# Infini-attention plus SiLU MLP: two input tiles loaded in halves on two queues, VectorE's constants made later, 39 idle products for 44

## The chip, the core and the metric

The kernel runs on one core of a Trainium2 chip. TensorE (PE, with its weight loads as PEld), VectorE (DVE), ScalarE (ACT), GpSimd (POOL) and SyncE (SP) each work through an order of their own; DMAs are issued by SP and ACT and carried by 16 DMA engines. The metric is device time in microseconds, lower is better. Three runs of the kernel before took 222.0, 222.07 and 222.56 us, median 222.07.

## What is computed

The input x is 2048 rows of 512 bf16 values. Each row is normed (mean and variance), and the normed rows go through an attention with memory and through a dense block; both results are added to x.

```
xn  = layernorm(x)
q, k, v = xn @ wq, xn @ wk, xn @ wv            # 32 heads of 16, 4 segments of 512 rows
a_dot = softmax(q k^T * scale + causal mask) v   # inside a segment
a_mem = (phi(q) M) / (phi(q) z)                # M, z: sums over the segments before
out = x + (g * a_mem + (1 - g) * a_dot) @ wo + silu(xn @ w1) @ w2
```

## The kernel before, in words

The rows are cut into 16 tiles of 128 rows, four to a segment. The order of all work is written out by hand in the string ORDER (L16 to L90): each word names a piece with its numbers, a table at L839 maps it to a function, and a loop at the end emits the pieces one after the other. Nothing reorders them; each engine gets its own instructions in that order and waits on semaphores only.

The first line of ORDER is the start of the kernel, and it is what the change touches. Its words, as far as they matter here:

- `kind`, `odd`, `omask` (L232, L217, L229): eight small VectorE instructions that make constants of one column: which rows are even or odd heads (pm_odd, pm_even), and masks worked out from them. pm_odd and pm_even are first read by GpSimd at L376, in the copy of the first keys; the others much later.
- `ones0`, `ones1`, `zeros`: memsets of GpSimd.
- `xc`t, `xd`t (L279, L283): the statistics of tile t on VectorE and their aggregation; `xq`t (L297) a square root on ACT, `xi`t (L300) the reciprocal, `Nv`t (L308) the normed tile xn_t, both on VectorE.
- `busy`n (L833): n idle products on PE, 128x128 by 128x128, of zeros; they read zraw, which VectorE's first memset fills, and write a bank that nobody reads. `busy44` stands ahead of the first turn, `busy6` behind it.
- `X`t`.1` (L812): four transposes of xn_t on PE into PSUM, and `Xa`, `Xv` (L819) their copies to xnT by ACT (tiles 0 and 1) or VectorE (tiles 2 and 3).
- `v0.0.`n, `v0.1.`n (L386): the value products of tiles 0 and 1, one product per word, which read wv; `k0.`, `q0.` (L365, L380) the keys and queries of the first segment, which read wk and wq and all four tiles; `tb` (L303) loads ACT's table for the exponential.
- `h` (L470): the dense block's products, which read w1.

Ahead of the loop, the function issues the input DMAs (L163 to L180). Tile 0 goes on SP's queue and tile 1 on ACT's, then tile 2 on SP's and tile 3 on ACT's; then SP issues wv in two parts, wk, wq, four tiles of x, w1, and the other eight tiles. A DMA's end is counted on one of eight counters, given out in turn: the ninth DMA of the program takes over that of an early one and is issued only once that one has ended. In the kernel before the ninth is the load of tiles 4 to 7 (x_hi), which waits for tile 1.

On VectorE the start is: memset of zraw (L183), memset of the lower half of lows (L257), the eight constants, then the statistics of tile 0. On ACT: two DMA issues, the load of the square root's table with a small activation (L185), then the square root of tile 0.

Of the kernel before, what the change touches and what calls it, by code (L numbers as in the profile page):

```python
# [13 lines left out]


ORDER = """  # L16
kind odd omask ones0 ones1 zeros xc0 xd0 xc1 xq0 xi0 Nv0 busy44 xd1 xq1 xc2 xi1 X0.1 Nv1 xd2 Xa0.1 busy6 v0.0.0 v0.0.1 xq2 X1.1 Xa1.1 xs3 v0.0.2 v0.0.3 xq3 v0.1.0 xi2 v0.1.1 v0.1.2 v0.1.3 Nv2 xi3 X2.1 va0.0 va0.1 Nv3 Xv2.1 X3.1 Xv3.1 k0.0.0 k0.0.1 k0.1.0 k0.0.2 k0.0.3 k0.3.0 q0.0.0 q0.0.1 q0.0.2 q0.0.3 ka0.0 fp0.0 qv0.0 tb fa0.0 q0.2.0 k0.1.1 k0.1.2 k0.1.3 kv0.1 fp0.1
S0 q0.1.0 q0.1.1 q0.1.2 q0.1.3 k0.3.1 xs4 xs6 xs7 xs5 xg4.4 q0.2.1 q0.2.2 qa0.1 q0.2.3 qv0.2
S2 v0.2.0 v0.2.1 k0.3.2 k0.3.3 kv0.3 fa0.1 v0.3.0 v0.3.1 v0.3.2 Nv7 v0.2.2 XD7 v0.2.3
S1 Nv5 vv0.2 h0.5.0 h0.10.0 h0.10.1 h0.10.2 v0.3.3 vv0.3 xs8 Nv6 XD6 h0.5.1 h0.5.2 XD5 h0.5.3 ha0.5  # L20
# [73 lines left out]
def kernel(  # L94
# [13 lines left out]
    nc = tc.nc  # L108

    P = 128  # L110
# [14 lines left out]
    x_flat = A_x.flatten_outer_dims()  # L125
# [18 lines left out]
    def xs(t0, t1):  # L144
        if t0 >= NT - TPS:
            return x_end[:, t0 - NT + TPS : t1 - NT + TPS, :]
        return x_lo[:, t0:t1, :] if t1 <= TPS else x_hi[:, t0 - TPS : t1 - TPS, :]
# [6 lines left out]
    wo_sb = cpool.tile([P, DT, D], BF16, name="wo_sb")  # L154
    beta_r = cpool.tile([P, 1], BF16, name="beta_r")

    def load_x(eng, t0, n):
        eng.dma_start(
            out=xs(t0, t0 + n),
            in_=x_flat[t0 * P : (t0 + n) * P, :].rearrange("(n p) d -> p n d", p=P),  # L160
        )

    load_x(nc.sync, 0, 1)  # L163
    load_x(nc.scalar, 1, 1)
    load_x(nc.sync, 2, 1)
    load_x(nc.scalar, 3, 1)
    def load_w(eng, w_sb, W, k0, k1):
# [11 lines left out]
        out=beta_r[:], in_=bass.AP(tensor=A_beta.tensor, offset=A_beta.offset, ap=[[1, H], [0, 4], [1, 1]])  # L179
# [9 lines left out]
    for i in range(2):  # L189
# [6 lines left out]
        out=b16[:], in_=ones8[:], compare_op=ALU.is_ge, fill=0.0,  # L196
# [3 lines left out]
        out=b16[:], in_=b16[:], compare_op=ALU.is_ge, fill=0.0,  # L200
# [9 lines left out]
    kind = cpool.tile([P, 1], F32, name="kind")  # L210
# [16 lines left out]
    omask = cpool.tile([P, 1], I32, name="omask")  # L227
# [687 lines left out]
```

## Time and profile before

| | us |
|---|---|
| median of three runs | 222.07 |
| the profiled execution's own time | 222.15 |
| its span, first to last instruction | 220.4 |
| PE busy, sum over the span | 214.9 (97%) |
| ACT busy | 184.0 (83%) |
| DVE busy | 179.7 (82%) |
| POOL busy | 135.1 (61%) |

The profile is that of one execution. Times in it count from the first instruction, so the 1.75 us between span and time lie around it. A row of the timeline has start, length, engine, line of the kernel, operation, tile written and tiles read, how many were merged, and in brackets how long the engine was idle before and what released it. SPq and ACTq are the queues that issue DMAs. In the rows on DMA queues stand packets, MB and the share of 16 engines; q1 is SP's queue and q10 ACT's. In the row of an instruction group, three numbers in ns are the least, median and greatest duration.

### The profile page before, as it was taken

How to read it: one execution, taken by the hardware profiler on the slowest of the kernel's cores; microseconds unless marked ns; L12 is line 12 of the kernel's file. 1: busy time of each engine (PE TensorE's matmuls, PEld its weight loads, DVE VectorE, ACT ScalarE, POOL GpSimd, SP SyncE). 2: the span in 40 equal slices, each digit the busy share in tenths (PEclk: the TensorE clock that was granted, in tenths of full speed). 3: DMA queues.
4: the chain of work that ended last, by engine and by line, in shares of the span. 5: the costliest groups of instructions: out<-in, count | busy, mean ns of one | idle time of the engine just before them, and what ended most of it. 6: DMA issues, size and time to landing. Idle time of an engine off the chain costs nothing.

```text
span 220.4 us, 9441 instructions
## 1 busy us (share of the span) xinstructions
PE 214.9 (97%) x4057; PEld 117.2 (53%) x4057; DVE 179.7 (82%) x368; ACT 184.0 (83%) x173; POOL 135.1 (61%) x253
## 2 busy tenths in 40 slices
PE   7999999999999999999999999999999999999994
PEld 7666645655553444454544444455454544455662
DVE  7789999988889788776897888969789887579554
ACT  3699999999999999999998999999989997971000
POOL 6089667997769976876669696693756364320000
PEclk9999999999999999999999999999999999999999
DMA  5993549552014221223303130142242020232313
GB/s 183 373 385 87 74 27 304 106 77 58 21 28 122 88 59 29 50 51 76 102 17 95 40 96 4 28 92 59 52 120 64 15 76 7 75 94 68 109 51 97
DMA packets 32746, 19.61 MB, mean 89 GB/s; under 512 B 14656, under 2 KB 32192, under 8 KB 32704
## 3 DMA queue, kind: packets, MB, share of 16 engines
q1 hardware_dynamic: 30080, 16.39, 28.6%
q10 hardware_dynamic: 2624, 2.62, 3.9%
q8 instruction: 31, 0.51, 1.0%
q14 instruction: 11, 0.09, 0.2%
HBM read 9.96 MB, written 2.10 MB: 55 GB/s over the span
## 4 chain that ended last, share of the span: by engine, by line
PE 79%; ACT 10%; DVE 4%; POOL 4%; issue 2%; POOLq 0%
PE ps L331 21%; PE psO L333 16%; PE ps L333 13%; PE psS L701 10%; PE psO L331 9%; ACT Pb L707 7%; PE psV L763 6%; PE psS L333 4%; POOL Pb L718 2%; DVE xn_t L310 1%; POOL lows L718 1%; ACT ex L408 1%; ACT th L477 1%; PE psM L437 1%; DVE stats L281 1%
## 5 line engine op out<-in xcount | busy, mean ns | idle before, releaser
L707 ACT ACTIVATE Pb<-psS 128x2048 bf16<-128x2048 f32 x72 | 135.2, 1878 | 7.5 <-PE psS L701 6.4
L718 POOL TENSOR_SCALAR_AFFINE_SELECT Pb<-Pb 128x256 bf16<-128x256 bf16 (+2 forms) x120 | 66.1, 571 | 22.3 <-ACT Pb L707 19.5
L482 DVE SCALAR_TENSOR_TENSOR hT<-th,ps 128x512 bf16<-128x512 bf16 x56 | 37.7, 679 | 9.1 <-ACT th L477 8.5
L718 POOL TENSOR_SCALAR_AFFINE_SELECT lows<-Pb 64x256 bf16<-64x256 bf16 (+1 forms) x56 | 26.7, 490 | 27.7 <-ACT Pb L707 25.3
L333 PE MATMUL psO<-w_sb,hT 128*32 128x512 bf16 (+2 forms) x716 | 42.5, 319 | 0.0
L331 PE MATMUL ps<-xnT,w_sb 128*128 128x512 bf16 (+1 forms) x160 | 35.2, 334 | 0.0
L477 ACT ACTIVATE th<-ps 128x512 bf16<-128x512 f32 x56 | 33.0, 598 | 2.2 <-PE ps L333 2.1
L333 PEld LDWEIGHTS <-hT 128*32 128x32 bf16 x884 | 21.8, 96 | 14.0 <-issue 3.3
L333 PE MATMUL ps<-xnT,w_sb 128*32 128x512 bf16 (+1 forms) x480 | 27.1, 341 | 0.1
L701 PE MATMUL psS<-qT,k 32*128 32x64 bf16 (+3 forms) x512 | 23.0, 233 | 0.8 <-ACT Pb L707 0.3
L331 PE MATMUL psO<-w_sb,hT 128*128 128x512 bf16 (+2 forms) x87 | 22.7, 334 | 0.0
L701 PEld LDWEIGHTS <-k 32*128 32x128 bf16 x512 | 9.8, 92 | 23.2 <-issue 21.7
L763 PE MATMUL psV<-Pb,Vz 128*32 128x448 bf16 (+7 forms) x512 | 21.6, 286 | 0.3 <-POOL Pb L718 0.3
L331 PEld LDWEIGHTS <-w_sb 128*128 128x128 bf16 x160 | 14.9, 98 | 12.1 <-issue 1.6
L763 PEld LDWEIGHTS <-Vz 128*32 128x32 bf16 x768 | 16.5, 97 | 9.1 <-issue 1.1
L376 POOL TENSOR_SCALAR k<-kT,pm_odd 128x512 bf16<-128x512 bf16 x16 | 12.0, 748 | 8.0 <-ACT kT L373 7.0
L333 PEld LDWEIGHTS <-w_sb 128*32 128x32 bf16 x480 | 11.9, 96 | 7.3 <-issue 1.9
L331 PE MATMUL ps<-wv_sb,xnT 128*128 128x512 bf16 x56 | 15.1, 381 | 0.2
L701 PE MATMUL psS<-qT,kT 16*128 16x448 bf16 (+3 forms) x256 | 14.7, 269 | 0.0
L333 PE MATMUL psO<-wo_sb,oT 128*32 128x512 bf16 x156 | 14.4, 380 | 0.0
L331 PE MATMUL ps<-xnT,wk_sb 128*128 128x256 bf16 (+1 forms) x64 | 13.6, 326 | 0.0
L793 DVE CAST oraw<-psV 128x512 bf16<-128x512 f32 x16 | 11.0, 689 | 3.0 <-PE psV L763 2.9
(110 smaller groups left out, 321.2 us busy)
## 6 DMA issues: line engine op xcount, KB each, us to landing
spr<-rz SPq DMA_DIRECT2D x56, 64.0 KB
x_res<-in_A_x_dram SPq DMA_DIRECT2D x16, 128.0 KB
out_dram<-o_out SPq DMA_DIRECT2D x15, 128.0 KB
w_sb<-in_B_w_dram SPq DMA_DIRECT2D x1, 1792.0 KB
w_sb<-in_B_w_dram ACTq DMA_DIRECT2D x1, 1792.0 KB
x_hi<-in_A_x_dram SPq DMA_DIRECT2D x2, 512.0 KB
wv_sb<-in_A_wv_dram SPq DMA_DIRECT2D x2, 256.0 KB
wk_sb<-in_A_wk_dram SPq DMA_DIRECT2D x1, 512.0 KB
```

Of the source, the lines that this page charges most:

```text
L281: nc.vector.bn_stats(out=stats[t][:], in_=xs(t, t + 1)[:, 0, :])
L310: eng.tensor_scalar(out=xn[t][:], in0=xs(t, t + 1)[:, 0, :], scalar1=mv_all[:, t, 0:1], scalar2=rstd_all[:, t, 0:1], op0=ALU.subtract, op1 ...
L331: return [nc.tensor.matmul(out, lhsT=lhsT, rhs=rhs, start=start, stop=stop, skip_group_check=True)]
L333: nc.tensor.matmul(out[c : c + 32], lhsT=lhsT[:, c : c + 32], rhs=rhs, start=start, stop=stop, tile_position=(0, c), skip_group_check=True,)
L376: nc.gpsimd.tensor_scalar(out=to, in0=frm, scalar1=keep[:, 0:1], scalar2=1.0, op0=ALU.mult, op1=ALU.mult)
L477: nc.scalar.activation(out=th[:], in_=sts[s]["h", ft][:, :], func=AF.Tanh, scale=0.5)
L482: nc.vector.scalar_tensor_tensor(out=st["hT"][:, ft, :], in0=st.pop(("th", ft))[:], scalar=1.0, in1=st.pop(("h", ft))[:, :], op0=ALU.add, ...
L701: nc.tensor.matmul(psS[:, g, c : c + q2 - q1], lhsT=keys[rows], rhs=st["qT"][rows, dt, q1:q2], start=True, stop=True, tile_position=(32 * ...
L707: exp = nc.scalar.activation(out=Pb[:, :, :], in_=psS[:, :, :], func=AF.Exp, scale=SCALE)
L718: over[id(Pb)].append(nc.gpsimd.affine_select(out=out, in_=in_, compare_op=ALU.is_ge, fill=0.0, base=base, pattern=[[0, out.shape[1]], [1, ...
L763: nc.tensor.matmul(psV[32 * g : 32 * g + 32, q0 : q0 + nq], lhsT=Vzs[s % 2][:, kt, 4 * dt + g, par : par + 2, :].rearrange("p a d -> p (a ...
L793: copy(out=oraw[:], in_=sts[s].pop(("psV", 0))[:, :])
```

## The change

Three edits at the start of the kernel. Tiles 0 and 1 are loaded by four DMAs for two: rows 0 to 63 of each on SP's queue, rows 64 to 127 on ACT's, tile 0 ahead of tile 1 on both. The eight constants of VectorE move from the head of ORDER to behind the copies of the turned tiles 2 and 3 (`Xv2.1`, `Xv3.1`), with `odd` now ahead of `kind`. And `busy44` becomes `busy39`. As two DMAs more come first, the ninth DMA of the program is now wk, which waits for the first half of tile 0; wq waits for its second half.

```diff
 ORDER = """
-kind odd omask ones0 ones1 zeros xc0 xd0 xc1 xq0 xi0 Nv0 busy44 xd1 xq1 xc2 xi1 X0.1 Nv1 xd2 Xa0.1 busy6 ...
-... Nv3 Xv2.1 X3.1 Xv3.1 k0.0.0 k0.0.1 ...
+ones0 ones1 zeros xc0 xd0 xc1 xq0 xi0 Nv0 busy39 xd1 xq1 xc2 xi1 X0.1 Nv1 xd2 Xa0.1 busy6 ...
+... Nv3 Xv2.1 X3.1 Xv3.1 odd kind omask k0.0.0 k0.0.1 ...
...
-    def load_x(eng, t0, n):
+    def load_x(eng, t0, n, rows=slice(0, P)):
         eng.dma_start(
-            out=xs(t0, t0 + n),
-            in_=x_flat[t0 * P : (t0 + n) * P, :].rearrange("(n p) d -> p n d", p=P),
+            out=xs(t0, t0 + n)[rows],
+            in_=x_flat[t0 * P : (t0 + n) * P, :].rearrange("(n p) d -> p n d", p=P)[rows],
         )
-    load_x(nc.sync, 0, 1)
-    load_x(nc.scalar, 1, 1)
+    for t in range(2):
+        load_x(nc.sync, t, 1, slice(0, P // 2))
+        load_x(nc.scalar, t, 1, slice(P // 2, P))
     load_x(nc.sync, 2, 1)
     load_x(nc.scalar, 3, 1)
```

More of the change, by code (lines that the diff above doesn't have):

```diff
@@ L16 @@
 ORDER = """
-kind odd omask ones0 ones1 zeros xc0 xd0 xc1 xq0 xi0 Nv0 busy44 xd1 xq1 xc2 xi1 X0.1 Nv1 xd2 Xa0.1 busy6 v0.0.0 v0.0.1 xq2 X1.1 Xa1.1 xs3 v0.0.2 v0.0.3 xq3 v0.1.0 xi2 v0.1.1 v0.1.2 v0.1.3 Nv2 xi3 X2.1 va0.0 va0.1 Nv3 Xv2.1 X3.1 Xv3.1 k0.0.0 k0.0.1 k0.1.0 k0.0.2 k0.0.3 k0.3.0 q0.0.0 q0.0.1 q0.0.2 q0.0.3 ka0.0 fp0.0 qv0.0 tb fa0.0 q0.2.0 k0.1.1 k0.1.2 k0.1.3 kv0.1 fp0.1
+ones0 ones1 zeros xc0 xd0 xc1 xq0 xi0 Nv0 busy39 xd1 xq1 xc2 xi1 X0.1 Nv1 xd2 Xa0.1 busy6 v0.0.0 v0.0.1 xq2 X1.1 Xa1.1 xs3 v0.0.2 v0.0.3 xq3 v0.1.0 xi2 v0.1.1 v0.1.2 v0.1.3 Nv2 xi3 X2.1 va0.0 va0.1 Nv3 Xv2.1 X3.1 Xv3.1 odd kind omask k0.0.0 k0.0.1 k0.1.0 k0.0.2 k0.0.3 k0.3.0 q0.0.0 q0.0.1 q0.0.2 q0.0.3 ka0.0 fp0.0 qv0.0 tb fa0.0 q0.2.0 k0.1.1 k0.1.2 k0.1.3 kv0.1 fp0.1
 S0 q0.1.0 q0.1.1 q0.1.2 q0.1.3 k0.3.1 xs4 xs6 xs7 xs5 xg4.4 q0.2.1 q0.2.2 qa0.1 q0.2.3 qv0.2
```

## The prediction

> **What bounds the kernel now.** I read first the table of busy time by stage, to see which stage the edit lies in, then the chain of waits from the start, then the timeline of the first 18 us by engine, and last the DMA counts in narrow windows. The stage table has the window, its length, and then busy time of PE, PEld, DVE, ACT and POOL:
>
> ```profile
> 13.00:33.00 20.00, 19.35 (x260) 11.96 (x259) 19.17 (x41) 19.92 (x19) 15.64 (x30) 1.00 0.55 118
> 33.00:215.00 182.00, 181.44 (x3629) 94.55 (x3631) 149.19 (x296) 156.81 (x140) 114.32 (x207) 1.00 0.28 71
> ```
>
> From 13 to 33 us ACT has no gap (19.92 of 20.00), and from 33 on PE has none (181.44 of 182.00). Nothing in the edit touches those stages, so all that it can do is to let them begin earlier or later; every engine runs a fixed order, so a shift that reaches 13 us goes through to the end. Only the start has room: until 5.7 us PE does idle products alone. The chain of waits (start, length, what) names who sets its end:
>
> ```profile
> 1.40 1.23 DVE lows L257
> 2.63 0.03 issue
> 2.66 0.23 DVE kind L234
> ...
> 3.52 0.12 DVE omask L230
> 3.64 0.01 issue
> 3.65 0.71 DVE stats L281
> ...
> 5.71 0.41 PE ptr L817 x4
> ...
> 10.60 0.59 ACT kT L373
> ```
>
> VectorE goes from the memset of lows without a gap through the constants (2.66 to 3.64) into the statistics of tile 0, and from there the chain is tile 0's norm, its turn, the first value products (at 6.56, a row below) and the first keys at 10.60. So the constants look like 1.0 us on the path. They are not, because tile 0 itself is only just there. Its landing has to be read from the packets. Five windows follow: 1.8 to 2.4 (both queues), 2.4 to 2.8 (both queues), 2.8 to 3.2, 3.2 to 3.3 and 3.3 to 3.4 us; q1 is SP's queue, q10 ACT's:
>
> ```profile
> q1 hardware_dynamic: 21, 0.02, 10.9%
> q10 hardware_dynamic: 4, 0.00, 3.3%
> q1 hardware_dynamic: 75, 0.08, 54.7%
> q10 hardware_dynamic: 55, 0.06, 39.4%
> DMA packets 176, 0.15 MB, mean 374 GB/s; under 512 B 30, under 2 KB 176, under 8 KB 176
> DMA packets 41, 0.04 MB, mean 410 GB/s; under 512 B 1, under 2 KB 41, under 8 KB 41
> DMA packets 37, 0.04 MB, mean 369 GB/s; under 512 B 1, under 2 KB 37, under 8 KB 37
> ```
>
> Tiles 0 and 1 are 128 packets of 1 KB each, one tile on each queue, and each ends in 16 packets under 512 B. Those 32 ends come as 30, 1 and 1: the last two fall in 3.2 to 3.3 and in 3.3 to 3.4. When is an end known to the engines? The timeline of the issuing queues and ACT tells it for tile 1:
>
> ```profile
> 0.79 0.87 SPq L158 DMA_DIRECT2D x_lo<-in_A_x_dram  x2
> 1.70 0.95 SPq L168 DMA_DIRECT2D wv_sb<-in_A_wv_dram  x2
> 1.71 1.28 ACT L185 ACT_TABLE_LOAD   x1 [1.71 <-PEq L899]
> 2.68 0.47 SPq L168 DMA_DIRECT2D wk_sb<-in_A_wk_dram  x1
> 3.20 0.51 SPq L168 DMA_DIRECT2D wq_sb<-in_A_wq_dram  x1
> 3.83 0.42 SPq L158 DMA_DIRECT2D x_hi<-in_A_x_dram  x1
> 4.66 0.29 ACT L298 ACTIVATE rstd_all<-mv_all,eps 128x1 f32<-128x1 f32 x1 [1.45 <-DVE mv_all L284]
> ```
>
> The ninth transfer of the program (x_hi) takes over the completion counter of tile 1 and waits for it. It starts 0.12 us behind the issue before it (3.20 + 0.51 = 3.71), where the others follow within 0.06. So tile 1 was done at about 3.8, some 0.45 behind its last end. The same lag behind the earlier end (3.2 to 3.3) puts tile 0 at 3.65 to 3.75, and as its statistics began at 3.65 it was there by then. Tile 0's landing and the last constant end within a few hundredths of each other: each covers the other, and taking either away alone gains almost nothing.
>
> **The change part by part.** *Constants (L217, L229, L232).* Eight instructions of VectorE, 2.66 to 3.64, leave the place ahead of the statistics; VectorE is then free at 2.63. They come back behind the copies of the turned tiles 2 and 3:
>
> ```profile
> 11.69 0.69 DVE L384 CAST qT<-ps 128x512 bf16<-128x512 f32 x1 [1.78 <-PE ps L331]
> 11.29 0.70 POOL L376 TENSOR_SCALAR k<-kT,pm_odd 128x512 bf16<-128x512 bf16 x1 [7.01 <-ACT kT L373]
> ```
>
> There VectorE idles 1.78 us, from 9.91 to 11.69, so 0.98 fit. GpSimd's first user of pm_odd starts at 11.29, and pm_odd and pm_even stand first of the eight (done some 0.3 us behind 9.91). Cost 0; without that gap it would be up to 0.98 on the first copy of queries.
>
> *Halves.* Both queues now carry 64 rows of tile 0 first, then 64 of tile 1; bytes per queue are the same. Now the 128th packet of q1, tile 0's last, goes near 3.0 (21 + 75 = 96 by 2.8, the other 32 at the 75 per 0.4 us of q1), 0.65 ahead of the statistics. No row shows a transfer of 64 rows, so bounds. Slowest: nothing is gained (3.63, as now). By each queue's present count, q10's 64th goes just behind 2.8 (4 + 55 = 59 by then): 2.82 + 0.65 = 3.47. If tile 0 had the whole flow, its 128 packets would be through when 25 of before 2.4 and 103 more at 130 per 0.4 us have gone, at 2.72, and by 0.65 for the end there at 3.37; with 0.45 behind its last end and no straggling one as that of 3.2 to 3.3, at 3.2. Tile 0's second half shares each engine with tile 1's first for part of the way, so I take the nearest row's count and the whole flow's as neighbours and 3.38 between them and the fast end: 0.27 earlier.
>
> The row first, then a rule: in these windows both queues share one flow of at most 410 GB/s. The Trainium skill (DMA: Bandwidth & Descriptors, Rules for kernel authors) says of two transfers to disjoint halves of the partitions that they aren't worth it, since both go over the same 16 engines. By it this term would be 0 and not 0.27. I don't follow it in full, because here the halves do not add bandwidth but move tile 0's second half ahead of tile 1.
>
> *Queued behind the halves.* Each queue issues one transfer more, 0.87 / 2 = 0.43 us. On ACT the table load goes from 1.71 to about 2.15 and ends at 3.43, its small activation follows; ACT's first root then waits for VectorE at about 4.3 as before (it idles 1.45 now): 0. Tiles 2 and 3 are used only behind tile 0's norm, which ends just ahead of 5.71: 0. On SP the first half of wv is issued at 2.13 for 1.70, and wk, which is now the ninth transfer, waits for the first half of tile 0, and wq for the second. wk is used at 9.21, and q1 had passed the bytes up to wk (1.31 MB) at 7.0; w1 is used at 17.76, and the bytes up to w1 (4.19 MB) were through before 15. The first three rows are q1 up to 4.9, 7.0 and 15; then the users, the idle products that start up to 4.7, those that run after it, the six later ones, and the least, median and greatest duration of one in ns:
>
> ```profile
> q1 hardware_dynamic: 573, 0.54, 34.8%
> q1 hardware_dynamic: 1344, 1.30, 55.4%
> q1 hardware_dynamic: 3124, 4.36, 82.0%
> 9.21 1.57 PE L331 MATMUL ps<-xnT,wk_sb 128*128 128x256 bf16 x12
> 17.76 1.05 PE L331 MATMUL ps<-xnT,w_sb 128*128 128x256 bf16 x8
> 6.56 0.11 PEld L331 LDWEIGHTS <-xnT 128*128 128x128 bf16 x2 [0.30 <-ACT xnT L823]
> 1.10 3.81 PE L836 MATMUL psS<-zraw 128*128 128x128 bf16 x34 [1.10 <-DVE zraw L183]
> 4.49 1.00 PE L836 MATMUL psS<-zraw 128*128 128x128 bf16 x12
> 5.94 0.50 PE L836 MATMUL psS<-zraw 128*128 128x128 bf16 x6
> L836 PE MATMUL psS<-zraw x50: 219/314/314, 1.1 to 6.2; 128*128 128x128 bf16 x50
> ```
>
> Both cost 0. The first half of wv is closer: the products that read it start at 6.56 behind ACT's copy, so it landed by then. With 0.27 gained they want it at 6.30. Its lateness lies between 0 and 0.43; it had landed somewhere from 5.5 (q1 had passed the bytes up to it, 0.52 MB, by 4.9, and 0.65 for the end) to 6.56. Middles: 6.05 + 0.2 = 6.25, just in time, so I charge 0.03 and keep up to 0.43 of loss against now for the range.
>
> *39 idle products for 44.* 34 start from 1.10 to 4.7, one each 0.107 us. The six later ones go at (0.50 - 0.22) / 5 = 0.056. The twelve from 4.49 end at 5.49, so the last starts at 5.27: 11 steps in 0.78, about three of the long kind and eight of the short, and the pace changes at 4.8. The 39th starts at 5.27 - 5 x 0.056 = 4.99. Tile 0's turn wants PE at 5.71 - 0.27 = 5.44, after both: 0. The cut matters from a gain of about 0.4 on, where 44 products would hold the turn up.
>
> Sum: -0.27 + 0.03 = -0.24 us. The profiled execution took 222.15 us (span 220.4 and 1.75 around it), the median of the runs is 222.07, 0.08 below. 222.07 - 0.24 = **221.8 us**.
>
> **The rivals.** *The full half microsecond:* tile 0 lands by 3.2 and wv in time. For it: the 25 packets before 2.4 are a slow start, and shorter transfers may fill the flow sooner. Against: q10's 4 among them. Gain 0.45 to 0.5, 221.6. *Nothing gained:* tile 0 lands when it did, as the two queues share one flow; VectorE then idles 1.0 us ahead of it. 222.05. The rule of the Trainium skill weighed above is this case. *wv late:* it may have landed at the late end of its bounds now, and then the issue put in front moves it by the whole 0.43 past 6.56; against it, q1 had passed its bytes at 4.9; 222.07 + 0.43 less 0.1 for the part that it was early, 222.4.
>
> *Slower:* PE's pace doubles at 4.8 us, after 3.7 us of products. 44 products reach 0.45 us past that point, 39 only 0.2. If the change of pace comes later than the products end, the eight first value products and sixteen turns go at half pace: the 8 at about 4 x 0.056 each (four times as wide) and the 16 at 0.056 make 2.7 us more, less the 0.30 gap of the row above; some 2.2 if all of them, 1.1 if half, less the 0.24. It decides from 0.2 us of lateness on: with half of them 222.07 + 1.1 - 0.24 = 222.95. The Trainium skill (TensorE: Matmul & The Clock Gate, Part 1) has the same 107 and 56 ns and says that the window that counts activity runs free and the point varies by half a microsecond; that would make this case real in some runs, not in most. No row here shows a second such point.
>
> **How the numbers follow.** Forecast (221.65 to 222.0) 0.41, full gain 0.21, nothing 0.15, wv late 0.09, late pace 0.14. The three runs before spread over 0.56 us, so each case is some 0.3 wide. 0.3% (about what a measurement of this kernel can tell from no change) is 0.67 us: faster means below 221.40, which three fifths of the full gain and a seventh of the forecast reach by scatter and by gains that I can't see; slower means above 222.74: late pace and half of wv late. Faster 0.19, same 0.62, slower 0.19. Range 221.2 to 222.9: it takes in all cases but most of the late pace and the fast edge.
>
> **What would show it.** Right: statistics of tile 0 at 3.2 to 3.5 behind an idle VectorE, the norm at about 5.0, the turn at 5.4, the keys' copy at 10.35, and the eight constants inside VectorE's gap from 9.7 on. Wrong: statistics at 3.6 (halves bring nothing), value products that start later than ACT's copy (wv), products at 0.107 us apart beyond 5 us (pace), or a start that is earlier and an end that isn't.

## The result

The changed kernel took 223.28 us (median of 8 runs, 222.79 to 224.02), the kernel before 222.1 beside it (8 runs, 221.98 to 222.72): a ratio of 1.0047, with a 95% interval of 1.0029 to 1.0065. The change costs about 1.1 us. The forecast was 221.8, and the time lies above its range too.

| us | before | after |
|---|---|---|
| median | 222.1 | 223.28 |
| the profiled execution | 222.15 | 222.84 |
| its span | 220.4 | 221.1 |

### The profile page after: what moved, and what is told of

It reads as the page before. It is cut to its first block, busy times and chain, and to the rows that moved or that the text cites. A ratio compares the mean times of both kernels' runs of the same rounds, so it can differ in the third digit from the quotient of the medians.

```text
span 221.1 us, 9410 instructions
## 1 busy us (share of the span) xinstructions
PE 213.2 (96%) x4027; PEld 117.5 (53%) x4052; DVE 179.3 (81%) x368; ACT 183.9 (83%) x173; POOL 135.3 (61%) x253
## 4 chain that ended last, share of the span: by engine, by line
PE 75%; ACT 10%; POOL 4%; DVE 3%; DMA 3%; issue 2%; SPq 1%; POOLq 0%
PE ps L332 19%; PE psO L334 16%; PE ps L334 13%; PE psS L702 9%; PE psO L332 8%; ACT Pb L708 8%; PE psV L764 6%; PE psS L334 4%; DMA wk_sb<-in_A_wk_dram 3%; POOL Pb L719 2%; SPq L158 1%; POOL lows L719 1%; DVE xn_t L311 1%; ACT ex L409 1%; ACT th L478 1%
## 5 line engine op out<-in xcount | busy, mean ns | idle before, releaser
L332 PE MATMUL ps<-xnT,w_sb 128*128 128x512 bf16 (+1 forms) x152 | 33.6, 332 | 0.4 <-DVE odd L801 0.2
L332 PE MATMUL psO<-w_sb,hT 128*128 128x512 bf16 (+2 forms) x82 | 21.3, 331 | 0.5 <-issue 0.3
L332 PE MATMUL ps<-wv_sb,xnT 128*128 128x512 bf16 x51 | 14.5, 380 | 0.7 <-ACT rstd_all L299 0.4
L332 PE MATMUL ps<-xnT,wk_sb 128*128 128x256 bf16 (+1 forms) x61 | 13.0, 324 | 0.6 <-DVE oraw L808 0.2
```

What stands on the lines that cost most here:

```text
L332: return [nc.tensor.matmul(out, lhsT=lhsT, rhs=rhs, start=start, stop=stop, skip_group_check=True)]
```

## The profile after

First the timeline of the changed kernel (start, length, engine, line, what, and in brackets the idle time before with its releaser):

```profile
0.79 2.12 SPq L158 DMA_DIRECT2D x_lo<-in_A_x_dram  x3
1.10 4.34 PE L837 MATMUL psS<-zraw 128*128 128x128 bf16 x39 [1.10 <-DVE zraw L184]
2.94 0.94 SPq L169 DMA_DIRECT2D wv_sb<-in_A_wv_dram  x2
3.34 0.69 DVE L282 BATCH_NORM_STATS2 stats<-x_lo 128x6 f32<-128x512 bf16 x1 [0.71 <-DMA x_lo<-in_A_x_dram]
3.94 0.47 SPq L169 DMA_DIRECT2D wk_sb<-in_A_wk_dram  x1
5.41 0.61 PE L818 MATMUL ptr<-ident,xn_t 128*128 128x128 bf16 x4
5.82 0.83 PE L837 MATMUL psS<-zraw 128*128 128x128 bf16 x6
7.00 0.38 PE L332 MATMUL ps<-wv_sb,xnT 128*128 128x512 bf16 x1 [0.36 <-ACT rstd_all L299]
9.88 1.21 PEld L332 LDWEIGHTS <-wk_sb 128*128 128x128 bf16 x12 [0.27 <-DMA wk_sb<-in_A_wk_dram]
9.89 1.48 PE L332 MATMUL ps<-xnT,wk_sb 128*128 128x256 bf16 x12
10.25 0.15 DVE L219 TENSOR_REDUCE pm_odd<-b 128x1 f32<-128x4 f32 x1
11.02 0.14 DVE L231 CAST omask<-pm_odd 128x1 int32<-128x1 f32 x1
11.88 0.69 POOL L377 TENSOR_SCALAR k<-kT,pm_odd 128x512 bf16<-128x512 bf16 x1 [7.60 <-ACT kT L374]
20.84 1.88 ACT L708 ACTIVATE Pb<-psS 128x2048 bf16<-128x2048 f32 x1
```

Down to the statistics it goes as the change means it: tile 0 is there at 3.34, 0.31 earlier than the 3.65 of before, VectorE idles 0.71 ahead of it, and the constants sit between 10.25 and 11.16 where nobody waits for them (pm_odd's reader, GpSimd, starts at 11.88 behind the copy of the keys). But the first value product comes at 7.00 where it was at 6.57, and the first keys at 9.89 where they were at 9.21. Something between took back the gain and more. The chain of waits of the same kernel (start, length, what) names it:

```profile
0.79 0.60 SPq L158
...
1.44 0.81 SPq L158
...
2.31 0.60 SPq L158
...
2.94 0.43 SPq L169
...
3.94 5.91 DMA wk_sb<-in_A_wk_dram
9.84 0.05 issue
9.89 1.28 PE ps L332 x10
```

It no longer runs over VectorE and the norm of tile 0, as before, but over SP's queue and a weight. Three issues of x take SP 0.60, 0.81 and 0.60 us. The rows of before had two in 0.87. So wv is issued at 2.94 for 1.70, wk at 3.94 for 2.68, and wk lands at 9.84, when PE has already idled for it.

The packed trace also keeps the counter of every transfer. It is raised sixteen times, and the last raise is the landing (for wk 9.84, as in the chain). Read so, the first half of wv landed at 6.00 in the kernel before, wk at 8.21 and w1 at 16.89; in the changed kernel they landed at 6.96, 9.84 and 18.24. So wv was late as well. The row at 7.00 names a root of ACT as what released the product, but the product doesn't read that root, and wv's counter was full 0.04 us ahead of it.

How far the shift goes is seen against two rows of the timeline of the kernel before, the first queries and the fourth exponential over scores:

```profile
10.62 1.25 PE L331 MATMUL ps<-xnT,wq_sb 128*128 128x256 bf16 x10
20.26 1.88 ACT L707 ACTIVATE Pb<-psS 128x2048 bf16<-128x2048 f32 x1
```

At 20 us the changed kernel is 0.58 behind (20.84 for 20.26), and its span ends 0.7 later. The stages behind are as full as they were; the changed kernel's busy times from 13 to 33 us (window, length, then PE, PEld, DVE, ACT, POOL) show ACT without a gap again:

```profile
13.00:33.00 20.00, 19.27 (x264) 11.92 (x265) 19.05 (x41) 19.91 (x21) 15.52 (x30) 1.00 0.57 149
```

So in this execution the loss is made in the first 10 us and carried to the end.

## The experiments

**Theories.** *Queue:* the loss comes from SP, which issues the weights over a microsecond later, because transfers of 64 rows take it long; the halves as such, the constants and the 39 products are innocent. Rivals: *pace* (the idle products are fewer, and the turn and the value products run at half pace), *constants* (they are now in somebody's way), and *halves* (transfers of half the partitions slow the DMA engines themselves).

Each run stands beside runs of the kernel before on the same chip. "wv" is the time at which SP began to issue wv in the profiled execution, "keys" the start of the first keys.

| kernel | wv | keys | median us | before | ratio (95%) |
|---|---|---|---|---|---|
| before | 1.70 | 9.21 | | | |
| the change again | 2.94 | 9.59 | 223.22 | 222.38 | 1.0046 (1.0024 to 1.0068) |
| halves alone | 2.94 | 9.60 | 223.26 | 222.38 | 1.0033 (1.0012 to 1.0054) |
| constants alone | 1.70 | 9.01 | 222.5 | 222.38 | 1.0001 (0.9985 to 1.0018) |
| 39 products alone | 1.71 | 9.19 | 222.25 | 222.38 | 0.9994 (0.9977 to 1.001) |
| change, tile 2 on ACT's queue | 2.31 | 9.14 | 222.59 | 222.39 | 1.0016 (0.9996 to 1.0036) |
| change, tile 0 alone in halves | 2.30 | 9.20 | 222.99 | 222.39 | 1.0028 (1.0008 to 1.0049) |
| change, halves by columns | 2.17 | 9.35 | 222.63 | 222.39 | 1.0005 (0.9991 to 1.0018) |
| change, tile 0 in halves, SP issues wv second | 1.45 | 9.21 | 222.34 | 222.35 | 0.9998 (0.9987 to 1.0009) |
| before, wv behind three tiny transfers | 3.12 | 9.19 | 223.39 | 222.39 | 1.0053 (1.0036 to 1.007) |
| whole tiles, tile 0 ahead of all | 1.70 | 8.88 | 221.83 | 222.39 | 0.9973 (0.9961 to 0.9985) |

### The three edits, each alone, and the change again

Halves alone: ORDER as before, with `busy44` and the constants in front.

```diff
 # halves alone, against the changed kernel
-ones0 ones1 zeros xc0 xd0 xc1 xq0 xi0 Nv0 busy39 ... Xv3.1 odd kind omask k0.0.0 ...
+kind odd omask ones0 ones1 zeros xc0 xd0 xc1 xq0 xi0 Nv0 busy44 ... Xv3.1 k0.0.0 ...
```

> The halves alone, constants in front and 44 idle products as before. Queue theory (the two transfers more keep wv and wk from being issued in time): nearly all of the loss is here, time 1.003 to 1.006 of before; the first keys' products start at 9.7 to 9.9 us for 9.21, the issues of x take 0.55 to 0.8 us each for 0.43, and the first product that reads wv starts at 6.9 or later. Pace theory (39 products end before PE's pace doubles): no loss, within 0.1% of before, as 44 products are there.

Constants alone, then 39 products alone, against the kernel before:

```diff
 # constants alone
-kind odd omask ones0 ... Xv3.1 k0.0.0 ...
+ones0 ... Xv3.1 odd kind omask k0.0.0 ...
 # 39 products alone
-... Nv0 busy44 xd1 ...
+... Nv0 busy39 xd1 ...
```

> The constants' move alone. Queue theory and pace theory: within 0.1% of before; tile 0's statistics start at 3.6 behind an idle VectorE, since the tile lands no earlier. Theory of the constants (they hold up the first keys or queries where they now stand): 0.2% or more slower, with an idle GpSimd or VectorE behind the eight at 10 to 11 us.

> 39 idle products for 44 alone. Queue theory: within 0.1% of before. Pace theory: 0.2 to 0.6% slower, with products still 0.107 us apart beyond 5.7 us.

The changed kernel once more, for a second profile:

> The changed kernel, unchanged, profiled a second time: 1.003 to 1.0065 of before. If the longer issues of x (0.56 to 0.81 us) and the late wk (first keys' products at 9.89) belong to the change, they are here again; if they were an accident of that execution, the issues are 0.4 to 0.46 and the loss lies elsewhere. PE's pace doubled at 6.4 there; if that point wanders by itself it is elsewhere here.

Halves alone carry the loss (1.0033, and the change again 1.0046, with intervals that overlap); the other two edits do nothing that can be told from zero. That ends the rival of the constants. The one profiled execution of halves alone was the slowest of its twelve, and its fourth exponential starts only 0.33 later than before (20.59); the rest of its loss comes late (below). The second profile of the change shows the wait more plainly than the first. Its timeline:

```profile
5.37 0.42 PE L818 MATMUL ptr<-ident,xn_t 128*128 128x128 bf16 x4
5.63 0.50 PE L837 MATMUL psS<-zraw 128*128 128x128 bf16 x6
6.25 0.10 PEld L332 LDWEIGHTS <-xnT 128*128 128x128 bf16 x1 [0.30 <-ACT xnT L824]
6.97 0.59 PE L332 MATMUL ps<-wv_sb,xnT 128*128 128x512 bf16 x2 [0.84 <-DMA wv_sb<-in_A_wv_dram]
9.59 1.57 PE L332 MATMUL ps<-xnT,wk_sb 128*128 128x256 bf16 x12
11.44 0.99 PEld L332 LDWEIGHTS <-wq_sb 128*128 128x128 bf16 x10 [0.56 <-DMA wq_sb<-in_A_wq_dram]
```

Here the gain of tile 0 reaches PE whole: the turn is at 5.37 for 5.71, and the turned rows are loaded into PE at 6.25 for 6.56. Then PE idles 0.84 us for wv. wk is in time here (its counter is full at 9.03, the keys start at 9.59), but wq is late (11.44, the first queries at 10.62 before). The turn and the six products run at full pace here (0.42 and 0.50), while in the first profile they took 0.61 and 0.83; the loss is there either way. So the pace is not its cause: that rival falls for the changed kernel. With 39 products alone the row of these products is as slow as one can be, and the first keys still start at 9.19:

```profile
1.10 4.34 PE L836 MATMUL psS<-zraw 128*128 128x128 bf16 x39 [1.10 <-DVE zraw L183]
```

### Fewer issues ahead of the weights

Tile 2 moves from SP's queue to ACT's; then, in another kernel, only tile 0 goes in halves and tile 1 whole on ACT's queue. Both leave SP one issue less.

```diff
 # tile 2 on ACT's queue
-    load_x(nc.sync, 2, 1)
+    load_x(nc.scalar, 2, 1)
 # tile 0 alone in halves
-    for t in range(2):
-        load_x(nc.sync, t, 1, slice(0, P // 2))
-        load_x(nc.scalar, t, 1, slice(P // 2, P))
+    load_x(nc.sync, 0, 1, slice(0, P // 2))
+    load_x(nc.scalar, 0, 1, slice(P // 2, P))
+    load_x(nc.scalar, 1, 1)
```

> The change with tile 2 on ACT's queue, so that SP issues wv as its third transfer again. Theory that late wv and wk carry the loss: wv is issued at 2.3 for 2.94 us, wk about 0.6 earlier, the first keys' products start at 9.3 or before for 9.6 to 9.9, time 1.001 to 1.003 of before. Theory that the 64-row transfers load the DMA engines themselves worse: as the change, 1.003 to 1.006, keys at 9.6 to 9.9.

> Only tile 0 in halves, tile 1 whole on ACT's queue; SP carries half of tile 0, tile 2, wv. If a transfer of 64 rows is what takes long to issue (0.56 to 0.82 for 0.40): one long issue on each queue, the others at 0.40 to 0.46; wv issued at 1.9, time within 0.15% of before. If long issues come from both queues issuing at once over a longer time: the whole tiles' issues are 0.5 to 0.6 too; wv at 2.0 to 2.3, time 1.001 to 1.003.

The weights are issued 0.63 us sooner than in the change (2.31 and 2.30), and the ratio falls from 1.0046 to 1.0016 and 1.0028, though the intervals overlap. The statistics still start early (3.32 and 3.43). Of the two expectations for the second kernel the first failed: the whole tile behind the half of 64 rows took SP 0.81 to issue, so that wv went out at 2.30 and not at 1.9. Its profiled execution took 222.3, well under its median of 222.99, and shows no late weight; what its other executions lost isn't in a profile.

### Halves without 64 rows

The halves are cut by columns: 128 partitions of 256 elements each. The number of transfers, their bytes and their order are those of the change.

```diff
-    def load_x(eng, t0, n, rows=slice(0, P)):
+    def load_x(eng, t0, n, cols=slice(0, D)):
...
-            out=xs(t0, t0 + n)[rows],
+            out=xs(t0, t0 + n)[:, :, cols],
...
-        load_x(nc.sync, t, 1, slice(0, P // 2))
-        load_x(nc.scalar, t, 1, slice(P // 2, P))
+        load_x(nc.sync, t, 1, slice(0, D // 2))
+        load_x(nc.scalar, t, 1, slice(D // 2, D))
```

> The change with halves by columns for rows: 128 partitions of 512 bytes each, the same four transfers. If 64 rows are what makes an issue long: issues of 0.40 to 0.46, wv issued at 2.1, time 1.000 to 1.002 of before. If the number of transfers in a row does it: issues of 0.55 to 0.8 as in the change, wv at 2.9, time 1.003 to 1.006.

Its chain of waits, with SP's issues one by one:

```profile
0.79 0.39 SPq L158
...
1.24 0.42 SPq L158
...
1.70 0.42 SPq L158
...
2.17 0.43 SPq L169
```

And its timeline at the statistics and the first keys:

```profile
3.10 0.69 DVE L282 BATCH_NORM_STATS2 stats<-x_lo 128x6 f32<-128x512 bf16 x1 [0.47 <-DMA x_lo<-in_A_x_dram]
9.35 1.49 PE L332 MATMUL ps<-xnT,wk_sb 128*128 128x256 bf16 x12 [0.52 <-DMA wk_sb<-in_A_wk_dram]
```

Same number of transfers, but each issue takes 0.39 to 0.42 where those of 64 rows took 0.60 and 0.81 and the whole tile behind them 0.60. wv goes out at 2.17, very near the 2.13 that the prediction had put, and the loss of the change is gone (1.0005). The length of the issues is thus the matter, and it comes with the 64 rows. The gain isn't there either: the statistics start 0.55 earlier than before, but PE waits 0.52 for wk, and the first keys start at 9.35, later than the 9.21 of before. wk, issued 0.48 later than before, now sets the first keys, and w1, whose counter is full at 18.20, sets what follows: at 20 us this execution (222.72) is 0.43 behind.

### 64 rows with the weights out early

Only tile 0 goes in 64-row halves, ACT takes all else of x, and SP issues wv right behind its half.

```diff
+    load_x(nc.sync, 0, 1, slice(0, P // 2))
+    load_x(nc.scalar, 0, 1, slice(P // 2, P))
+    for t in range(1, 4):
+        load_x(nc.scalar, t, 1)
```

> The change with only tile 0 in halves of 64 rows and tiles 1, 2 and 3 whole on ACT's queue, so that SP issues wv as its second transfer. Theory that the loss is late wv and wk: wv issued at 1.45 to 1.7, statistics at 3.4, first product that reads wv at 6.3, first keys' products by 9.1, time 0.998 to 1.0005 of before, though a 64-row transfer leads both queues. Theory that 64-row transfers cost beyond their issue: 1.002 or more.

```profile
0.79 0.60 SPq L158 DMA_DIRECT2D x_lo<-in_A_x_dram  x1
1.45 1.32 SPq L168 DMA_DIRECT2D wv_sb<-in_A_wv_dram  x2
3.43 0.69 DVE L281 BATCH_NORM_STATS2 stats<-x_lo 128x6 f32<-128x512 bf16 x1 [0.80 <-DMA x_lo<-in_A_x_dram]
5.48 0.61 PE L817 MATMUL ptr<-ident,xn_t 128*128 128x128 bf16 x4
5.88 0.68 PE L836 MATMUL psS<-zraw 128*128 128x128 bf16 x6
9.21 1.57 PE L331 MATMUL ps<-xnT,wk_sb 128*128 128x256 bf16 x12
```

In this timeline both queues lead with 64 rows, and there is no loss: 0.9998. Its first issue takes 0.60 again, and the two issues of wv behind it 1.32 for 0.95. This kernel has only one such transfer on each queue, so by itself it doesn't end the rival of the halves; the counters do. From issue to landing wk took 5.1 to 6.0 us in the four profiles with halves of 64 rows of both tiles (the three of the change and that of halves alone), and 5.3 to 6.2 in the five that issue wk whole at 2.68 or 2.69, as before. wk is thus late by its issue and not by slower engines.

There is no gain either, though the statistics start 0.22 earlier and no weight is late. PE used the 0.22 up: the turn took 0.61 and the six products 0.68, where before they took 0.40 and 0.50, and the first value product starts at 6.55 for 6.57. The kernel with tile 0 alone in halves shows the same (0.61 and 0.55, then 6.56). So the pace doesn't make the loss of the change, but it can take a gain of this size.

### Late weights without halves

The test from the other side: the kernel before, whole tiles, 44 products, constants in front, with three tiny transfers (128 partitions of 32 bytes) put on SP's queue ahead of wv. They write where wo's own load writes later. Three executions of this kernel were profiled.

```diff
     load_x(nc.scalar, 3, 1)
+    for i in range(3):
+        nc.sync.dma_start(out=wo_sb[:, 0, i * DH : (i + 1) * DH], in_=x_flat[0:P, i * DH : (i + 1) * DH])
```

> The kernel before with three tiny transfers (128 x 32 bytes each, into a part of wo that is overwritten long after) on SP's queue ahead of wv; whole tiles, constants in front, 44 products. They put wv and wk off by as much as the change does (wv issued at about 2.95 for 1.70, wk at 4.1 for 2.68) without a 64-row transfer. Theory that late wv and wk are the whole loss: first product that reads wv at 6.9 to 7.1, first keys' products at 9.6 to 10.0, time 1.003 to 1.006 of before. Theory that 64-row transfers cost beyond their issue time: 1.001 or less.

> The kernel with three tiny transfers ahead of wv, unchanged, a further profile. Its first profile was that of its fastest execution (222.43 us, keys at 9.19) while its median was 223.39. Theory that late wv and wk carry the loss: in an execution near the median the first product that reads wv or the keys' are late by 0.4 to 1.0 against 6.57 and 9.21, and the shift is kept to the end. Other theory: the start is on time and the loss comes late, between 195 and 212 us.

> As the look before, once more, so that one of the two is likely to be an execution near the median of 223.39: same expectations.

The ratio is 1.0053: late weights without halves make a loss of the same size as the change. The tiny transfers also put some 400 small packets ahead of wv, so the run doesn't tell late issues from busier engines. The first profiled execution was the fastest of twelve (222.43) and shows next to nothing: wk issued at 4.23, keys at 9.19, 0.08 behind at 20 us. The second one took 223.16, and its chain of waits is that of the change:

```profile
4.15 5.91 DMA wk_sb<-in_A_wk_dram
10.06 0.05 issue
10.11 1.28 PE ps L333 x10
```

The keys start 0.90 later than before, and the fourth exponential 0.80 later (21.06 for 20.26). The third took 225.43: keys at 10.55, then w1 late too, and another 1.4 us at about 211 us, where VectorE waits 1.45 for a small DMA of the tail. The profiled execution of halves alone (224.37) lost 1.3 there in the same way. The three profiles of the change and that of before have no such wait there; why it comes now and then wasn't found.

One expectation failed: the first value product was to come at 6.9 to 7.1. It came at 6.55, 6.87 (with PE at half pace) and 6.48, and wv never held it up, although it was issued later than in the change. So this test shows the loss by late wk and w1, not by wv.

A third profile of the change was taken to see how the loss differs from one execution to the next:

> The changed kernel, a third profile. Theory of late wv and wk: shift of the first exponentials over the attention scores by 0.4 to 1.0 against 13.13 and kept to the end; issues of x at 0.56 to 0.82 us again. Other theory: part of the loss comes between 195 and 212 us, where one execution with halves lost 1.4.

```profile
18.84 1.05 PE L332 MATMUL ps<-xnT,w_sb 128*128 128x256 bf16 x8 [0.34 <-DMA w_sb<-in_B_w_dram]
21.29 1.87 ACT L708 ACTIVATE Pb<-psS 128x2048 bf16<-128x2048 f32 x1
```

This execution took 223.39; its keys started at 9.97, and w1 was late too, so that the fourth exponential stood 1.03 behind that of before. In the second profile as well the chain of waits runs over w1, which lands at 18.48, and no longer over wk:

```profile
5.56 12.92 DMA w_sb<-in_B_w_dram
18.48 0.05 issue
```

The three profiles line up: 0.58, 0.72 (20.98) and 1.03 us behind at 20 us, and executions of 222.84, 223.09 and 223.39, which are 0.69, 0.94 and 1.24 above the 222.15 of before. The late weights account for the loss but for some 0.1 to 0.2 us, which isn't traced.

### Tile 0 early without halves

Whole tiles, but tile 0 alone at the head: SP issues tiles 0 and 1, ACT first loads its table and then issues tiles 2 and 3. Constants moved, 39 products.

```diff
+    zraw = cpool.tile([P, L // 2], BF16, name="zraw")
+    nc.vector.memset(zraw[:], 0.0)
+    spare = cpool.tile([P, 1], F32, name="spare")
+    nc.scalar.activation(out=spare[:], in_=zraw[:, 0:1], func=AF.Sqrt)
     load_x(nc.sync, 0, 1)
-    load_x(nc.scalar, 1, 1)
-    load_x(nc.sync, 2, 1)
+    load_x(nc.sync, 1, 1)
+    load_x(nc.scalar, 2, 1)
     load_x(nc.scalar, 3, 1)
...
-    zraw = cpool.tile([P, L // 2], BF16, name="zraw")
-    nc.vector.memset(zraw[:], 0.0)
-    spare = cpool.tile([P, 1], F32, name="spare")
-    nc.scalar.activation(out=spare[:], in_=zraw[:, 0:1], func=AF.Sqrt)
```

> Whole tiles, constants moved, 39 idle products; tile 0 and tile 1 on SP's queue, tiles 2 and 3 on ACT's behind its table load, so that tile 0 has the engines to itself and SP issues wv when it did before. Queue theory: tile 0's statistics at 3.2 to 3.35, wv issued at 1.70, first keys' products at 8.9 to 9.0 for 9.21, time 0.998 to 0.9995 of before. If wv or wk were already the bound before the change: an earlier start and keys at 9.2, time as before.

```profile
1.70 0.94 SPq L172 DMA_DIRECT2D wv_sb<-in_A_wv_dram  x2
2.85 0.69 DVE L281 BATCH_NORM_STATS2 stats<-x_lo 128x6 f32<-128x512 bf16 x1 [0.22 <-DMA x_lo<-in_A_x_dram]
6.01 0.38 PE L331 MATMUL ps<-wv_sb,xnT 128*128 128x512 bf16 x1 [0.18 <-DMA wv_sb<-in_A_wv_dram]
8.88 1.48 PE L331 MATMUL ps<-xnT,wk_sb 128*128 128x256 bf16 x12
```

The timeline keeps SP's issues where they were (wv at 1.70) and has tile 0 at 2.85, 0.80 earlier. This one beats both kernels: 221.83 us, 0.9973 (0.9961 to 0.9985) of before. Of the 0.80 the first keys keep 0.33, because they start right behind the landing of wk, which the chain of this kernel gives:

```profile
2.68 6.16 DMA wk_sb<-in_A_wk_dram
8.84 0.05 issue
```

So wk, issued at 2.68 as before, lands at 8.84 here (8.21 in the profile of before). That bounds what an earlier tile 0 can bring.

Two variants of it: the constants back in front, and wk in two parts.

```diff
 # constants in front
-ones0 ... Xv3.1 odd kind omask k0.0.0 ...
+kind odd omask ones0 ... Xv3.1 k0.0.0 ...
 # wk in two parts
-    load_w(nc.sync, wk_sb, A_wk, 0, 4)
+    load_w(nc.sync, wk_sb, A_wk, 0, 2)
+    load_w(nc.sync, wk_sb, A_wk, 2, 4)
```

> Tile 0 first on SP's queue, but the constants in front of the statistics as before the change. Theory that the tile's landing and the constants cover each other: statistics at 3.65, no gain, 0.9995 to 1.0005 of before. Theory that only the tile's landing counts: as with the constants moved, 0.996 to 0.9985.

> Tile 0 first on SP's queue (as in the run before that won) with wk loaded in two halves, as the keys wait for it there (8.84 landed, 8.88 first product). Theory that keys wait for the whole of wk though their first products read only its first half: first keys' products at 8.7, wq later by the issue, time 0.996 to 0.9975 of before. Theory that the issue put in front of wq and the flow cancel it: 0.997 to 0.999, the wait is at the queries or the second part.

With the constants in front the median was 222.13 beside 222.39, 0.9991 (0.9972 to 1.0011): no gain that can be told from none. Two rows of its timeline:

```profile
3.48 0.15 DVE L230 CAST omask<-pm_odd 128x1 int32<-128x1 f32 x1
3.55 0.68 DVE L281 BATCH_NORM_STATS2 stats<-x_lo 128x6 f32<-128x512 bf16 x1
```

The statistics stand behind the last constant. With the constants moved and tile 0 as before (the second kernel of all) they wait 0.82 us for tile 0:

```profile
3.45 0.69 DVE L281 BATCH_NORM_STATS2 stats<-x_lo 128x6 f32<-128x512 bf16 x1 [0.82 <-DMA x_lo<-in_A_x_dram]
```

Neither brings a gain alone that can be told from none; both together bring 0.27%. wk in two parts gave 221.99, 0.9991 (0.9972 to 1.0009); its profiled execution took 222.42 with keys at 9.34. Against the kernel that it varies that settles nothing.

## Why the prediction was wrong

**Right.** *Tile 0's landing:* 3.38 was forecast for the statistics, and the three profiles have 3.34, 3.31 and 3.38. In part that is luck: the forecast took a middle between two bounds and reckoned with ACT's half as the later one, but in the changed kernel ACT's half landed at 2.93 and SP's at 3.25, as q1 had moved no packet by 2.4 us (21 before). *The two covers* (constants and landing hide each other): shown by the constants alone, and by the early tile with and without them. *The constants' new place:* 0, as reckoned. *39 products:* 0. *The wait of wk on a half of tile 0:* nothing, as SP issues wk 0.05 behind wv. (The half is not the one that was named: by the counters wk waits for rows 64 to 127, on ACT's queue, and wq for rows 0 to 63.) *wv before the change:* 6.05 was assumed, and its counter is full at 6.00. *A shift that reaches 13 us goes through:* it did, with 0.1 to 0.2 more.

**The step that failed** is "Queued behind the halves", first of all its figure for the issue: "Each queue issues one transfer more, 0.87 / 2 = 0.43 us". The issue of 64 rows was priced by that of 128, although the text itself had said that no row shows a transfer of 64 rows, and it bounded only the landing, not the issue. SP needed 1.24 us more (2.94 for 1.70): 0.18 and 0.38 for the long issues of the halves and 0.17 for the tile behind them, with the 0.43 of a third issue and the gaps. By columns, with issues of 0.39 to 0.42, wv was out at 2.17: there the 0.43 would have been right, and the loss was gone.

**The second part of the same step:** "Both cost 0", of wk and w1, since q1 had passed wk's bytes by 7.0 while wk was wanted at 9.21. Bytes passed in the sum over 16 engines are not a landing. In the changed kernel q1 has carried the same 1.31 MB by 8.5 us (its packets, MB and share up to then):

```profile
q1 hardware_dynamic: 1371, 1.31, 54.0%
```

and wk lands at 9.84, 1.34 us later: the sixteen raises of its counter run from 7.76 to 9.84. In the kernel before wk landed at 8.21, so the margin to 9.21 was 1.0 us and not 2.2, and that of w1 (16.89 to 17.76) 0.9 and not the 2.8 from 15. They would have borne the 0.43 of the prediction; they didn't bear 1.24. Nor are they fixed: with wk issued at 2.68 or 2.69 five profiles have it land at 7.96 to 8.84. By columns, issued 0.48 later, it landed at 9.31, behind its reader, and the forecast gain didn't come.

**The terms, as measured** in the three profiles of the change, each as the distance from before that has come together by then. At the statistics -0.27 to -0.34, for -0.27 forecast. At the first value product +0.29 to +0.43, where 0.03 had been charged for wv. At the first keys +0.38 to +0.76, where 0 had been charged for wk. At 20 us, with wq and w1, +0.58 to +1.03, for -0.24 forecast; in the second and third profile w1 sets it, for which 0 had been charged as well.

**The rivals.** *wv late* (222.4) had the right mechanism at the right place, but its condition, a wv that lands late already, wasn't met (6.00); its size was bounded by one issue of 0.43, and it stopped at wv where wk, wq and w1 hang on the same queue. *Late pace* was the case on the slow side, and the pace did wander, but the loss doesn't follow it. (Its sum was a little off: 2.7 less 0.30 is 2.4 and not 2.2.) *Nothing gained*, which is where the rule of the Trainium skill (DMA: Bandwidth & Descriptors, Rules for kernel authors) led, missed the landing: tile 0 did come 0.3 us earlier. Its advice to use one transfer over 128 partitions was right here, for another reason than the shared engines that it gives: the time on the issuing queue.

## What to carry to other kernels

At the head of a kernel, put down for each queue when every transfer behind an edit is issued and by when its reader wants it, and take a margin only from a landing that a wait or a counter shows, not from bytes passed. An issue of a shape that the trace doesn't have is a cost to bound like any other. Where two things cover each other, move both or neither, and look at once for the third that bounds them (here wk).

## What the runs showed of the hardware

An issue of 64 rows of 1 KB took 0.56 to 0.82 us of SP's or ACT's queue, and one of 128 partitions right behind them 0.59 to 0.81; elsewhere the tiles of x took 0.39 to 0.48 each, with rows of 512 bytes as with rows of 1 KB. What makes it longer wasn't tried. The Trainium skill (DMA: Bandwidth & Descriptors, Issuing engines are not separate DMA queues) says that the time to start a transfer is usually small beside the transfer; here 1.24 us of it cost 0.5% of the kernel.

From issue to landing of wk took 5.91, 6.16 and 5.91 us in three kernels where a chain shows it, and less than 4.96 in the fastest execution of the late weights (issued at 4.23, used at 9.19). A late issue is therefore not late in every execution, and one profile can miss what the median shows. The sixteen raises of one transfer's counter are far apart: for wk 1.2 us before (7.03 to 8.21) and 2.1 in the changed kernel.

PE's change of pace isn't fixed at 4.8 us: 39 products from 1.10 took 4.34 us in the changed kernel and 3.65 in the early tile's with constants in front, and 44 took 4.88 with late weights.
